# Sigmoid attention and a swish MLP on one core: layer one by seven products of halves, layer two in the same form, attention paced by batch

## The chip, the cores and the metric

One Trainium2 chip, one core. The metric is the device time of one execution in microseconds (us), as the median of several runs; the profile is of one further execution, on the same core. The engines are called by their short names: PE (TensorE, matrix products), DVE (VectorE), ACT (ScalarE), POOL (GpSimd, which also issues the casting loads) and SP (which issues the stores).

## The reference

```python
batch, n_heads, seq, head_dim = (8, 12, 448, 64)
n_tokens, d_model, d_ff = (3584, 768, 2048)

def _attn_ref(q, k, v):
    scale = 1.0 / np.sqrt(q.shape[-1])
    scores = scale * np.matmul(q, k.transpose(0, 1, 3, 2)) - np.log(S)
    attn = 1.0 / (1.0 + np.exp(-scores))
    return np.matmul(attn, v).astype(np.float32)

def _moe_ref(x, w_in, w_out, beta):
    h = x @ w_in
    g = h * (1.0 / (1.0 + np.exp(-beta * h)))
    return (g @ w_out).astype(np.float32)
```

Attention's output, heads side by side, is x: 8 batches of 448 tokens with 768 features. "Layer one" is h and g, 2048 features; "layer two" is the product with w_out, back to 768. All tensors come in float32; products run in float16 with float32 sums.

## The kernel before

**Attention.** Four heads are one quad, three quads a batch, 24 in all. A quad's q and k are loaded by POOL (tile `raw`), turned by DVE (`qT`, `kT`), and scored in visits (L218 on): one visit is 8 or 16 small products into two score tiles, which ACT turns into weights (`attnT`, L211, 128x896 at a time). There are two score tiles, so a visit's products wait for the sigmoids of the visit before. `attend` (L250 on) multiplies the weights of a whole quad by v, 16 products, and DVE casts the two results into `xT`, the batch's x with features on partitions.

**Layer one** (`dense1`, L280 on). For each of 16 blocks of 128 hidden features: six products of 128x128 weights by 448 tokens into one PSUM bank, one ACT sigmoid with beta as scale (L292), one DVE multiply of bank and sigmoid into `gt` (L295). In batch 0 the tokens are taken in two halves of 224. `gt` holds the hidden features of two batches.

**Layer two.** Tiles of 128 tokens. Tiles 0, 1, 2 and 27 are done directly (`dense2`, 16 products of 384 columns per half of the output). The others are done in pairs by Strassen's scheme (`strassen`, L377 on): the pair's hidden features, split in two halves, are a 2x2 matrix of blocks, w_out is another, and seven block products take the place of eight. Its weight sums (`weight_sum`) are made once by DVE, its five hidden sums per pair by DVE as they come up (L385), and the products are combined by DVE in `osb` (L415, L420) with one copy by ACT (L418).

**Banks.** PSUM has eight banks: four for the two score tiles, four single ones handed out by `bank`, the least recently used first. A product that has to stay open holds its bank by name (`held`) until `release`.

**Order.** The program order of every engine is written by hand. Attention's visits are the frame; between them stand units of a list, `fill` (layer one of a batch, then layer two of the tiles that it completes), each with an estimated cost in us. A visit is followed by units until their cost reaches a goal; the goals are a fixed list for the first visits (`spread`) and after them one rate for all. A batch's layer one has a first quad from which on it may start (`ready`). `attend` takes two banks, so units are run ahead of it until few enough are held. Engines run their queues in order; a wait holds back all that stands behind it on that engine.

The steps of the prediction touch `dense1` and its lines L284, L292, L295; `strassen`, L385 to L420; `attend` and L275; `bank`, `held`; `fill_units`, and the loop over visits at the end.

Of the kernel before, what the change touches and what calls it, by code (L numbers as in the profile page):

```python
# [13 lines left out]
def kernel(  # L14
# [17 lines left out]
    P = 128  # L32
# [23 lines left out]
    qTp = ctx.enter_context(tc.tile_pool(name="qTp", bufs=4))  # L56
    kTp = ctx.enter_context(tc.tile_pool(name="kTp", bufs=4))
    attnp = ctx.enter_context(tc.tile_pool(name="attnp", bufs=12))
    xTp = ctx.enter_context(tc.tile_pool(name="xTp", bufs=3))
    sump = ctx.enter_context(tc.tile_pool(name="sump", bufs=3))  # L60
    sigp = ctx.enter_context(tc.tile_pool(name="sigp", bufs=3))
# [31 lines left out]
    beta_in = const.tile([BLK, P], FP32, name="beta_in")  # L93
# [115 lines left out]
    def weigh(sco, n: int):  # L209
        at = attnp.tile([P, 2, S], FP16, tag="attnT", name="attnT")  # L210
        nc.scalar.activation(  # L211
            out=at[:, :, 0:n],
            in_=sco[:, :, 0:n],
            func=AF.Sigmoid,
            bias=NEG_LOG_S,
            scale=MSCALE,
        )
        return at  # L218
# [18 lines left out]
    def half_visit(g: int, c0: int, second: int):  # L237
# [13 lines left out]
        ats = {id(sco): weigh(sco, n) for sco, n in zip(scos, widths)}  # L251
# [53 lines left out]

    def dense2(t: int, half: int, part: int):
        last = t == NT - 1
        mid = 512 if last else HALF
        lo, hi = (0, mid) if half == 0 else (mid, DM)
        if part == 0:  # L310
            m2s[t, half] = bank("m2_ps", hi - lo, (t, half))
        m2 = m2s[t, half]
        for dc in range(part * NDC // N2, (part + 1) * NDC // N2):
            nc.tensor.matmul(  # L314
                m2,
                gt[:, dc, cols(t)],
                w_out16[:, dc, lo:hi],
                start=(dc == 0),
                stop=(dc == NDC - 1),
            )  # L320
        if part < N2 - 1:
            return
        release((t, half))
        if half == 0:
            osbs[t] = outp.tile([P, DM], FP32, tag="osb", name="osb")
        osb = osbs[t]
        nc.vector.tensor_copy(out=osb[:, lo:hi], in_=m2)  # L327
        if last:
            store(t, lo, hi)
        elif half == 1:  # L330
            store(t, 0, DM)
# [3 lines left out]
    def cols(t: int):  # L335
# [3 lines left out]

    ND = NDC // 2  # L340
    B11, B12, B21, B22 = (
# [4 lines left out]
    ws = {  # L346
        name: const.tile([P, ND, HALF], FP16, name=f"w_{name}")
        for name in ("T1", "T3", "T4", "T6", "T7")
    }

    def weight_sum(name: str, part: int):
        x, y, op = {
            "T1": (B11, B22, ALU.add),
            "T3": (B12, B22, ALU.subtract),
            "T4": (B21, B11, ALU.subtract),
            "T6": (B11, B12, ALU.add),
            "T7": (B21, B22, ALU.add),
        }[name]
        rows = slice(part * ND // 2, (part + 1) * ND // 2)
        nc.vector.tensor_tensor(out=ws[name][:, rows], in0=x[:, rows], in1=y[:, rows], op=op)  # L360
# [4 lines left out]

    def product(t: int, i: int):
        A11, A12, A21, A22 = hid(t, 0), hid(t, 1), hid(t + 1, 0), hid(t + 1, 1)
        return (
            ("r", A11, None, None, ws["T3"]),
            ("a", A22, None, None, ws["T4"]),  # L370
            ("s", A11, A12, ALU.add, B22),
            ("b", A21, A22, ALU.add, B11),
            ("a", A11, A22, ALU.add, ws["T1"]),
            ("r", A21, A11, ALU.subtract, ws["T6"]),
            ("a", A12, A22, ALU.subtract, ws["T7"]),
        )[i]

    NPROD = 7
    sums = {}

    def hidden_sum(t: int, i: int):
        _, x, y, op, _ = product(t, i)
        if op is not None:
            sums[t, i] = sump.tile([P, ND, P], FP16, tag="sum", name="sum")
            nc.vector.tensor_tensor(out=sums[t, i], in0=x, in1=y, op=op)  # L385

    def strassen(t: int, i: int, part: int):
        name, x, _, op, w = product(t, i)
        if part == 0 and i + 2 < NPROD:
            hidden_sum(t, i + 2)  # L390
        first = (t, name) not in m2s
        if first:
            m2s[t, name] = bank("m2_ps", HALF, (t, name))
        m2 = m2s[t, name]
        for dc in range(part * ND // 2, (part + 1) * ND // 2):
            nc.tensor.matmul(  # L396
                m2,
                (x if op is None else sums[t, i])[:, dc],
                w[:, dc],
                start=first and dc == 0,  # L400
                stop=(dc == ND - 1),
                skip_group_check=i >= 4,
            )
            first = False if dc else first
        if part == 0:
            return
        if i == 0:
            for u in (t, t + 1):
                osbs[u] = outp.tile([P, DM], FP32, tag="osb", name="osb")
        L, R = slice(0, HALF), slice(HALF, DM)  # L410
        o1, o2 = osbs[t], osbs[t + 1]
        r, a = m2s.get((t, "r")), m2s.get((t, "a"))

        def add(out, in0, in1, op=ALU.add):
            nc.vector.tensor_tensor(out=out, in0=in0, in1=in1, op=op)  # L415

        if i == 1:
            nc.scalar.copy(out=o2[:, L], in_=a)  # L418
        elif i == 2:
            nc.vector.tensor_copy(out=o1[:, L], in_=m2)  # L420
            add(o1[:, R], r, o1[:, L])
            release((t, "s"))
        elif i == 3:
            add(o2[:, L], m2, o2[:, L])
            release((t, "b"))
        elif i == 4:
            add(o2[:, R], a, o2[:, L], ALU.subtract)
        elif i == 5:
            add(o2[:, R], r, o2[:, R])
            release((t, "r"))  # L430
            store(t + 1, 0, DM)
        elif i == 6:
            add(o1[:, L], a, o1[:, L], ALU.subtract)
            release((t, "a"))
            store(t, 0, DM)
# [16 lines left out]
    M1_US, M1H_US, M2_US, LEAST_US = 1.13, 0.58, 2.6, 2.0  # L452


    def second_layer(tiles):
        for t in tiles:
            if t < 3 or t == NT - 1:
                for half in range(2):
                    for part in range(N2):
                        yield M2_US / N2, lambda a=(t, half, part): dense2(*a), False  # L460
            elif t % 2:
                for i in range(NPROD):
                    for part in range(2):
                        yield M2_US / 4, lambda a=(t, i, part): strassen(*a), i in (2, 3) or (i, part) == (4, 0)

    def filler_stream():
        for c0 in (0, QH):
            for dc in range(NDC):
                if c0 and dc == 10:
                    for part in range(N2):  # L470
                        yield M2_US / N2, 0, lambda part=part: dense2(0, 0, part), False
                yield M1H_US, 0, lambda dc=dc, c0=c0: dense1(0, dc, c0, QH), False
        for t, half in ((1, 0), (2, 0), (0, 1), (1, 1), (2, 1)):
            for part in range(N2):
                yield M2_US / N2, 0, lambda a=(t, half, part): dense2(*a), False
        for b in range(1, B):
            for dc in range(NDC):
                yield M1_US, QPB * (b + 1), lambda b=b, dc=dc: dense1(b, dc), False
            ends = [((x * S // P) - 1) // 2 * 2 + 1 for x in (b, b + 1)]
            for cost, unit, opens in second_layer(range(ends[0], NT if b == B - 1 else ends[1])):  # L480
                yield cost, 0, unit, opens

    fill = list(filler_stream())
    at_fill = [0]

    def fill_units(n: int):
        for _ in range(n):
            fill[at_fill[0]][2]()
            at_fill[0] += 1

# [3 lines left out]
    with tc.manual_schedule():  # L494
# [5 lines left out]
        still = const.tile([P, 512], FP16, name="still")  # L500
        nc.vector.memset(still, 0.0)
        nc.vector.memset(beta_in, 0.0)
# [64 lines left out]
        for g in range(QPB + 1, NQUAD, 2):  # L567
# [4 lines left out]
        spread += [2.95] * (sum(g < 4 * QPB for g, _, _ in visits) - len(spread))  # L572

        total = sum(u[0] for u in fill[at_fill[0] :])
        tail = 16 * M1_US + 9.6 * M2_US
        rest = (total - sum(spread) - tail) / (len(visits) - len(spread))
        adds = {
            5: [("T4", 0)],
            6: [("T4", 1)],
            8: [("T3", 0)],  # L580
            9: [("T3", 1), ("T1", 0)],
            10: [("T1", 1), ("T6", 0)],
            11: [("T6", 1)],
            12: [("T7", 0)],
            13: [("T7", 1)],
        }
        budget, spent = 0.0, 0.0
        for i, (g, jt, also) in enumerate(visits):
            if jt == 0:
                if g > QPB:  # L590


                    while len(held) > 1 and (len(held) > 2 or fill[at_fill[0]][3]):
                        spent += fill[at_fill[0]][0]
                        fill_units(1)
                    attend(g - 1, 0, S)
                if g + 2 < NQUAD:
# [9 lines left out]
            for name, part in adds.get(i, ()):  # L607
                weight_sum(name, part)
            budget += spread[i] if i < len(spread) else rest
# [6 lines left out]
            goal = max(budget, spent + LEAST_US) if g > QPB + 2 else budget  # L616
            while at_fill[0] < len(fill):
                cost, ready, _, _ = fill[at_fill[0]]
                if ready > g or spent + cost / 2 > goal:
                    break  # L620
                spent += cost
                fill_units(1)
        attend(NQUAD - 1, 0, S)
        fill_units(len(fill) - at_fill[0])
# [30 lines left out]
```

## Time and profile before

| | us |
|---|---|
| median of three runs | 387.97 (387.73 to 388.02) |
| profiled execution | 388.37 |
| its span, first to last instruction | 386.6 |
| layer-one products, 448 columns, 672 of them (L284) | 134.2 busy |
| attention sigmoids (L211), 171 of them | 145.2 busy |
| layer-one sigmoids (L292), 144 of them | 84.4 busy |
| POOL elementwise work | none but four small fills |

Busy time of PE is that of overlapping instructions: one product of 448 columns is shown as 353 ns while the next starts 189 ns after it. Starts, not durations, give PE's pace. The busy share of another engine is an average over stages: ACT is at 59% over the span and three quarters in layer one beside attention.

### The profile page before, as it was taken

The numbers are of one execution on the slowest core, as the hardware profiler recorded it, in microseconds if no ns is written. First come the engines' busy times: TensorE is split into PE (matmuls) and PEld (weight loads), VectorE is DVE, ScalarE is ACT, GpSimd is POOL, SyncE is SP. The second block draws the span as 40 slices with busy tenths as digits, with TensorE's granted clock in tenths as the row PEclk, the third lists the DMA queues.
The fourth block names the chain that finished last, engine by engine and source line by source line (L and its number), as shares of the span: only waits on it lengthen the run. The fifth ranks groups of instructions, "written<-read, shape, count | busy, mean of one in ns | idle before, by whom it ended". The sixth has DMA issues, their size and how long they took to land.

```text
span 386.6 us, 7375 instructions
## 1 busy us (share of the span) xinstructions
PE 381.2 (99%) x2991; PEld 191.4 (50%) x2991; DVE 231.5 (60%) x437; ACT 228.8 (59%) x329; POOL 67.3 (17%) x116
## 2 busy tenths in 40 slices
PE   8999999999999999999999999999999999999996
PEld 2478754444544444444554445544455444555563
DVE  2356364885766656565765667655686565645762
ACT  3987755687374795497364783467762677525200
POOL 7833353131110410140110410104100000000000
DMA  7999999728353850555363561639203300030033
GB/s 111 174 190 203 197 205 198 163 59 96 49 110 70 130 72 0 123 71 57 49 126 75 83 70 28 129 73 129 36 13 83 83 1 2 0 83 0 2 81 122
DMA packets 42401, 34.30 MB, mean 89 GB/s; under 512 B 21872, under 2 KB 38784, under 8 KB 42368
## 3 DMA queue, kind: packets, MB, share of 16 engines
q0 software_dynamic: 36976, 22.81, 43.6%
q1 hardware_dynamic: 5392, 11.02, 10.9%
q8 instruction: 23, 0.38, 0.4%
q14 instruction: 10, 0.08, 0.1%
HBM read 45.62 MB, written 11.01 MB: 146 GB/s over the span
## 4 chain that ended last, share of the span: by engine, by line
PE 95%; ACT 2%; DMA 1%; issue 1%; DVE 1%; POOL 0%; ACTq 0%; POOLq 0%
PE m_ps L284 38%; PE m_ps L396 29%; PE sco L200 12%; PE av_ps L266 10%; PE m_ps L314 5%; ACT attnT L211 2%; DMA raw<-in_k_dram 1%; PE idle_ps L507 1%; DVE xT L275 0%; POOL raw L110 0%; DVE kT L186 0%; ACT sg L292 0%; DVE osb L327 0%; DVE gt L295 0%; ACTq L292 0%
## 5 line engine op out<-in xcount | busy, mean ns | idle before, releaser
L211 ACT ACTIVATE attnT<-sco 128x896 f16<-128x896 f32 (+1 forms) x171 | 145.2, 902 | 89.1 <-PE sco L200 88.3
L284 PE MATMUL m_ps<-xT,w_in 128*128 128x448 f16 (+1 forms) x864 | 154.7, 332 | 0.2 <-DVE gt L295 0.2
L295 DVE TENSOR_TENSOR gt<-m_ps,sg 128x448 f16<-128x448 f32 (+1 forms) x144 | 81.7, 572 | 81.1 <-ACT sg L292 77.2
L284 PEld LDWEIGHTS <-w_in 128*128 128x128 f16 x864 | 80.6, 98 | 70.7 <-issue 15.3
L292 ACT ACTIVATE sg<-m_ps,beta_sb 128x448 f32<-128x448 f32 (+1 forms) x144 | 84.4, 596 | 36.3 <-PE m_ps L284 31.0
L396 PEld LDWEIGHTS <-sum 128*128 128x128 f16 x480 | 45.2, 98 | 36.2 <-issue 7.9
L200 PE MATMUL sco<-qT,kT 32*128 32x448 f16 (+3 forms) x864 | 52.2, 340 | 0.9 <-DVE kT L186 0.5
L396 PE MATMUL m_ps<-w_T,sum 128*128 128x384 f16 x288 | 51.6, 327 | 0.0
L110 POOL DMA_DIRECT2D raw<-in_q_dram x27 | 14.9, 553 | 186.5 <-DVE kT L190 180.2
L415 DVE TENSOR_TENSOR osb<-m_ps,osb 128x384 f32<-128x384 f32 x60 | 33.3, 555 | 18.7 <-PE m_ps L396 16.9
L266 PE MATMUL av_ps<-attnT,v 128*64 128x448 f16 (+3 forms) x432 | 42.1, 341 | 0.0
L275 DVE CAST xT<-av_ps 128x448 f16<-128x448 f32 (+1 forms) x54 | 28.8, 567 | 18.2 <-PE av_ps L266 18.2
L385 DVE TENSOR_TENSOR sum<-gt 128x1024 f16<-128x1024 f16 x60 | 39.1, 677 | 0.1
L396 PE MATMUL m_ps<-w_T,gt 128*128 128x384 f16 x192 | 34.2, 327 | 0.0
L396 PE MATMUL m_ps<-w_out,sum 128*128 128x384 f16 x192 | 33.7, 326 | 0.0
L266 PEld LDWEIGHTS <-v 128*64 128x64 f16 (+1 forms) x432 | 19.0, 108 | 24.6 <-issue 17.6
L200 PEld LDWEIGHTS <-kT 32*128 32x128 f16 (+1 forms) x864 | 13.5, 96 | 29.2 <-issue 27.0
L396 PEld LDWEIGHTS <-gt 128*128 128x128 f16 x192 | 18.1, 98 | 14.7 <-issue 3.1
L314 PE MATMUL m_ps<-w_out,gt 128*128 128x384 f16 (+2 forms) x128 | 22.5, 327 | 0.0
L131 POOL DMA_DIRECT2D v<-in_v_dram x32 | 19.8, 635 | 10.4 <-DMA w_in<-in_moe_w_in_dram 5.9
L178 DVE STREAM_TRANSPOSE qT<-raw 128x448 f32<-128x448 f32 (+1 forms) x27 | 16.6, 616 | 7.4 <-DMA raw<-in_q_dram 7.4
L314 PEld LDWEIGHTS <-gt 128*128 128x128 f16 x128 | 11.9, 98 | 10.3 <-issue 3.1
(23 smaller groups left out, 97.2 us busy)
## 6 DMA issues: line engine op xcount, KB each, us to landing
out_dram<-osb SPq DMA_DIRECT2D x98, 96.0 KB, 1.9
raw<-in_k_dram POOLq DMA_DIRECT2D x24, 224.0 KB, 4.7
raw<-in_q_dram POOLq DMA_DIRECT2D x21, 224.0 KB, 3.7
v<-in_v_dram POOLq DMA_DIRECT2D x32, 144.0 KB, 6.1
w_in<-in_moe_w_in_dram POOLq DMA_DIRECT2D x8, 384.0 KB, 10.9
w_out<-in_moe_w_out_dram POOLq DMA_DIRECT2D x4, 768.0 KB, 13.9
v<-in_v_dram POOLq DMA_DIRECT2D x16, 48.0 KB, 6.0
out_dram<-osb SPq DMA_DIRECT2D x2, 384.0 KB, 2.3
```

What stands on the lines that cost most here:

```text
L131: nc.gpsimd.dma_start(out=vs[b][i * BLK : (i + 1) * BLK, :, 0:JF].rearrange("p h j d -> p h (j d)"), in_=rows[:, :, JF * i * D : JF * (i + ...
L200: nc.tensor.matmul(sco[base : base + nk, hh, u0 : u0 + n], kT[g][lo : lo + BLK, jt * P : jt * P + nk, e], qT[g][lo : lo + BLK, c0 : c0 + n ...
L211: nc.scalar.activation(out=at[:, :, 0:n], in_=sco[:, :, 0:n], func=AF.Sigmoid, bias=NEG_LOG_S, scale=MSCALE,)
L266: nc.tensor.matmul(av[hh * D : (hh + 1) * D, 0:n], vs[b][base : base + nk, 2 * (s % NPAIR) + hh, jt], at[base : base + nk, hh, 0:n], start ...
L275: nc.vector.tensor_copy(out=xTs[b][:, s % NPAIR, c0 : c0 + n], in_=av[:, 0:n])
L284: nc.tensor.matmul(m1[:, 0:n], w_in16[:, hc, dc * P : (dc + 1) * P], xTs[b][:, hc, c0 : c0 + n], start=(hc == 0), stop=(hc == NHC - 1),)
L292: nc.scalar.activation(out=sg[:, 0:n], in_=m1[:, 0:n], func=AF.Sigmoid, bias=0.0, scale=beta_sb[:, dc : dc + 1])
L295: nc.vector.tensor_tensor(out=gt[:, dc, off : off + n], in0=m1[:, 0:n], in1=sg[:, 0:n], op=ALU.mult)
L314: nc.tensor.matmul(m2, gt[:, dc, cols(t)], w_out16[:, dc, lo:hi], start=(dc == 0), stop=(dc == NDC - 1),)
L385: nc.vector.tensor_tensor(out=sums[t, i], in0=x, in1=y, op=op)
L396: nc.tensor.matmul(m2, (x if op is None else sums[t, i])[:, dc], w[:, dc], start=first and dc == 0, stop=(dc == ND - 1), skip_group_check= ...
L415: nc.vector.tensor_tensor(out=out, in0=in0, in1=in1, op=op)
```

## The change

**Layer one of batches 2 to 7** (`wino1`). The features of x (768) and the tokens of a batch (448) are each cut in two halves, and so are the hidden features (2048). One 2x2 by 2x2 block product then takes seven products of halves (Winograd's form) in place of eight. A batch is four blocks d; each block makes 2 x 128 hidden features of the upper half and the same of the lower half by seven units in the order P1, P6, P5, P7, P2, P3, P4. A unit is six products of 224 columns. Four token sums (`token_sum`, DVE) are made per batch, queued in `side` and taken one after each unit, all of them ahead of P6. Four weight sums S1 to S4 are made once, S3 in the place of a block of w_in.

Three banks stay open across units: P2 adds to P1's bank, P3 to P5's, P4 to P7's. ACT copies P1 into an `osb` tile; DVE adds P6, P5, P7, P3 and P4 to what stands there. The sigmoids are on halves (two of 224 after P2, two of 224 after P3) and two of 448 after P4; one multiply of a block is DVE's, three are POOL's.

**Layer two** (`wino2`) is in the same form and order: four hidden sums a pair in place of five, five DVE adds, two ACT copies in place of one copy each by ACT and DVE. The pairs are 4-5 to 26-27, the direct tiles 0 to 3; T1 takes the place of a block of w_out. The last pair is stored in halves.

**Pacing.** From batch 2 on the goals rise evenly to the point at which the next batch's attention ends: two units before its layer one begins.

**Room.** `qT` and `kT` have 3 buffers (4 before), `attnT` 9 (12), `sg` 4 (3). Four of batch 0's attention tiles lie in `osb` tiles, and `still` and `beta_in` in other tiles.

```diff
-    qTp = ctx.enter_context(tc.tile_pool(name="qTp", bufs=4))
-    kTp = ctx.enter_context(tc.tile_pool(name="kTp", bufs=4))
-    attnp = ctx.enter_context(tc.tile_pool(name="attnp", bufs=12))
+    qTp = ctx.enter_context(tc.tile_pool(name="qTp", bufs=3))
+    kTp = ctx.enter_context(tc.tile_pool(name="kTp", bufs=3))
+    attnp = ctx.enter_context(tc.tile_pool(name="attnp", bufs=9))
...
+    ORDER = ("P1", "P6", "P5", "P7", "P2", "P3", "P4")
+    BANK = {"P1": "x", "P2": "x", "P6": "y", "P5": "w", "P3": "w", "P7": "z", "P4": "z"}
+    OPENS = ("P1", "P6", "P5", "P7")
...
+    def token_sum(b: int, i: int):
...
+        out, in0, in1 = (
+            (t[:, 0], b12, b11),
+            (t[:, 1], b22, t[:, 0]),
+            (b12, b22, b12),
+            (t[:, 2], b21, t[:, 1]),
+        )[i]
+        add(out, in0, in1, ALU.subtract)
...
+    def wino1(b: int, d: int, p: str):
+        while p == "P6" and side:
+            side.pop(0)()
...
+            "P1": lambda: (A11, x[:, 0:NK, 0:QH]),
+            "P2": lambda: (A12, x[:, NK:NHC, 0:QH]),
+            "P3": lambda: (S4, x[:, NK:NHC, QH:S]),
+            "P4": lambda: (A22, t[:, 2]),
+            "P5": lambda: (S1, t[:, 0]),
+            "P6": lambda: (S2, t[:, 1]),
+            "P7": lambda: (S3, x[:, 0:NK, QH:S]),
...
+        if opens:
+            m2s[key] = bank("m1_ps", S, key)
+        m = m2s[key].rearrange("p (q n) -> p q n", q=2)
+        for j in range(2):
+            for hc in range(NK):
+                nc.tensor.matmul(
+                    m[:, j],
+                    lhs[:, hc, (2 * d + j) * P : (2 * d + j + 1) * P],
+                    rhs[:, hc],
...
+        if p == "P1":
+            nc.scalar.copy(out=oa[:, 0], in_=m)
+        elif p == "P6":
+            add(oa[:, 0], m, oa[:, 0])
+        elif p == "P5":
+            add(oa[:, 1], m, oa[:, 0])
+        elif p == "P7":
+            add(oa[:, 1], m, oa[:, 1])
+        elif p == "P2":
+            for j in range(2):
+                sigmoid(ob[:, 1, j], m[:, j], 2 * d + j)
+        elif p == "P3":
+            add(ob[:, 0], m, oa[:, 0])
+            sg = sigp.tile([P, S], FP32, tag="sg", name="sg").rearrange("p (q n) -> p q n", q=2)
+            for j in range(2):
+                sigmoid(sg[:, j], ob[:, 0, j], 2 * d + j)
+            nc.gpsimd.tensor_tensor(
+                out=gt[:, 2 * d : 2 * d + 2, off + QH : off + S], in0=ob[:, 0], in1=sg, op=ALU.mult
+            )
+        elif p == "P4":
+            add(oa[:, 0], m, oa[:, 0])
+            first = m2s[b, d, "x"].rearrange("p (q n) -> p q n", q=2)
+            nc.vector.tensor_tensor(
+                out=gt[:, 2 * d : 2 * d + 2, off : off + QH], in0=first, in1=ob[:, 1], op=ALU.mult
+            )
+            release((b, d, "x"))
+            for j in range(2):
...
+                sigmoid(sg, oa[:, :, j], dc)
+                nc.gpsimd.tensor_tensor(
...
+        if p not in ("P1", "P5", "P7", "P2"):
+            release(key)
...
+        if p == "P1":
+            nc.scalar.copy(out=o2[:, L], in_=m2)
+        elif p == "P6":
+            add(o2[:, L], m2, o2[:, L])
+        elif p == "P5":
+            add(o2[:, R], m2, o2[:, L])
...
+        elif p == "P2":
+            nc.scalar.copy(out=o1[:, L], in_=m2)
...
+    def attended(g: int):
+        b, t = divmod(g, QPB)
+        if b > 1 and t == QPB - 1:
+            side.extend(lambda i=i: token_sum(b, i) for i in range(4))
...
-        spread += [2.95] * (sum(g < 4 * QPB for g, _, _ in visits) - len(spread))
-
-        total = sum(u[0] for u in fill[at_fill[0] :])
-        tail = 16 * M1_US + 9.6 * M2_US
-        rest = (total - sum(spread) - tail) / (len(visits) - len(spread))
...
+        for b in range(2, B):
+            knot = [v[:2] for v in visits].index((QPB * (b + 1), 0)) if b < B - 1 else len(visits)
+            n, at = knot - len(goals), goals[-1]
+            goals += [at + (starts[QPB * (b + 1)] - at) * (j + 1) / n for j in range(n)]
```

## The prediction

> **What bounds the kernel now.** I read the busy shares first, then the chain of waits, then the timeline of TensorE, and only then the other engines in the stages that the change rebuilds.
>
> ```profile
> PE 381.2 (99%) x2991; PEld 191.4 (50%) x2991; DVE 231.5 (60%) x437; ACT 228.8 (59%) x329; POOL 67.3 (17%) x116
> ...
> PE 95%; ACT 2%; DMA 1%; issue 1%; DVE 1%; POOL 0%; ACTq 0%; POOLq 0%
> ```
>
> TensorE (PE) is busy all the time and the chain that ends last is 95% PE. A busy PE need not be at full pace, so I take its pace from starts in its timeline:
>
> ```profile
> 39.51 2.47 PE L284 MATMUL m_ps<-xT,w_in 128*128 128x224 f16 x24
> 41.91 0.57 PE L200 MATMUL sco<-qT,kT 32*128 32x448 f16 x8
> 42.42 1.32 PE L284 MATMUL m_ps<-xT,w_in 128*128 128x224 f16 x12
> 43.58 0.65 PE L314 MATMUL m_ps<-w_out,gt 128*128 128x384 f16 x3
> ...
> 341.79 18.32 PE L284 MATMUL m_ps<-xT,w_in 128*128 128x448 f16 x96
> 359.94 2.76 PE L396 MATMUL m_ps<-w_T,gt 128*128 128x384 f16 x16
> ```
>
> Start to start, 96 products of 448 columns take 18.15 us: 0.189 us each. Those of 224 columns exist too (batch 0): 12 in 1.16 us, 0.097 each, and 24 in 2.40 us, 0.100 each with the 0.1 us in it that every switch to a score block costs. So half the columns cost about half, and nothing waits. The cover is in two windows: layer one of batch 3 between its score blocks, and of batch 7 alone.
>
> ```profile
> 122.60:148.70 26.10, 26.10 (x197) 11.53 (x197) 14.86 (x27) 19.94 (x29) 5.80 (x10) 1.00 0.62 93
> 341.80:360.00 18.20, 18.20 (x98) 9.43 (x97) 9.62 (x16) 9.50 (x15) 0.00 (x0) 1.00 0.12 28
> ```
>
> The columns are span, PE, weight loads, VectorE (DVE), ScalarE (ACT), POOL, clock, DMA. ACT is already 19.9 of 26.1 us in layer one with attention: three quarters. It hides because each layer-one unit needs one sigmoid and one multiply and then frees its bank.
>
> **The change, step by step.**
> (1) PE work. Batches 2 to 7 lose 6 x 96 = 576 products of 448 columns, 576 x 0.189 = 108.9 us, and gain 6 x 4 x 7 x 6 = 1008 of 224. At 0.096 (between the two rows, the switch taken off) that is 96.8 us: **-12.1 us**. Bounds: at 0.100 -8.1, at 0.0954 ((2.40 - 0.11)/24) -12.7. Layer two has seven products of the same size before and after, and the four tiles done directly are 0 to 3 in place of 0 to 2 and 27: nothing.
>
> The Trainium skill ("TensorE: Matmul & The Clock Gate", section "LDWEIGHTS (loading the stationary operand)") gives a weight load of P columns as P / 1.2 ns, an estimate of 107 ns for 128, more than a half product streams; were that the pace, the new products would take 107.5 us and the gain be 1.4. The trace has 24 such pairs in 2.40 us, so the loads overlap here and the rule does not bind.
>
> (2) ACT, per d (one block of seven products; four to a batch). Before, four sigmoids of 448. After: copy of P1 (the 384 copy takes 0.48; 0.53 for 448), two sigmoids of 224 after P2, two after P3, two of 448 after P4. Queue spacing, from runs in the rows: 224 0.34 (four in 1.47 us), 448 0.53, attention's 896 0.81 (two in 1.72).
>
> ```profile
> 134.65 0.63 ACT L292 ACTIVATE sg<-m_ps,beta_sb 128x448 f32<-128x448 f32 x1 [0.50 <-PE m_ps L284]
> 135.18 1.72 ACT L211 ACTIVATE attnT<-sco 128x896 f16<-128x896 f32 x2
> 136.77 1.39 ACT L292 ACTIVATE sg<-m_ps,beta_sb 128x448 f32<-128x448 f32 x2
> ```
>
> Sum 0.43 + 4 x 0.34 + 2 x 0.53 = 2.85 us per d, 11.4 a batch (8.5 before). In the built program's order four to six score blocks stand among a batch's 28 units, each with 1.62 us of ACT: about 20 us of ACT in a section whose PE work is 16.1 + 5 x 0.52 + 1.57 (one attend) = 20.2. **ACT becomes full where PE is full.**
>
> (3) The chain through one d. P2 adds to the bank that the copy of P1 reads; P3 to the bank of P5, after P5's add; P4 to that of P7. So PE itself waits now. ACT is in order: the next d's copy stands behind the P4 sigmoids of this one. From P4's last product to the next P3: drain 0.17 (a product's 0.35 less its slot of 0.19), add 0.62 (the 448 row of L295, 624 ns), two sigmoids 1.06, copy 0.53, add 0.62, add 0.62, four hand-overs of 0.03 (364.05 + 0.56 to 364.64): 3.74 us. PE has P1, P6, P5, P7, P2 to do meanwhile, 2.87. **It stands 0.87 us per d**, less 0.5 if a score block falls in between; and then two attention sigmoids (1.62) may stand in ACT's queue ahead of the copy.
>
> I walked the queues by hand in the built order with these durations. Batch 7, alone, from P1 of d0 at 1.30: copy 2.04 to 2.57; P3 at 5.24; P4 ends 6.39; its sigmoids 7.31 to 8.37; copy 8.90; P6's add 9.55, P5's 10.2; P3 at 10.24. So 5.0 us from P3 to P3 in place of 4.03, three times. Batch 4, with scores behind P6: d0's P4 sigmoids leave ACT at 6.51, the score block's two at 8.13, the copy ends at 8.66; P2 wanted 7.33 and goes at 8.70, P3 waits again to 10.0; d2 and d3 lose 0.5 to 1.3 each.
>
> (4) Token sums. P6 needs two of the four (672 elements; 1024 take 0.677, 1536 take 0.932, hence 0.50). They stand behind attend's two casts (1.16). With two units of layer two and P1 as cover P6 still waits 0.5 to 1.3 a batch. In the last batch a hidden sum adds 0.75 before layer two.
>
> Waits by batch, with (3) and (4): b2 3.0, b3 4.1, b4 5.5, b5 4.1 (the order of b3), b6 2.4, b7 4.9: **+24.0**.
>
> (5) Costed at nothing: six more weight sums (932 ns each) beside batch 1, where DVE is busy 16.0 of 23.7 us (window 75.0 to 98.7); without cover 5.6. Three multiplies a d on POOL: no row shows one; the same shape takes 0.62 on DVE and ACT's longest row is 0.915, and up to 1.34 each they fit in 4.03; I take 0.9 by the nearer engines. Queued behind them on POOL are the loads of raw and v, each issue 0.55 to 0.63 and landing in 4 to 6 us, a quad (some 12 us) before use; if POOL is late, the transposes on DVE are next and then the adds. The shorter rings (attnT 9, kT and qT 3) still hold a quad and the visit after it. osb is shared with layer two; d1 reuses tiles whose stores (1.9 us to land) left about 4 us earlier: nothing, 1 us a batch if not. I left the transposes (1.45 us a quad on DVE) out of the walk, 0 to 1 a batch more.
>
> The Trainium skill ("SBUF — State Buffer", section "SBUF: two separate sides") says that a VectorE instruction with two SBUF inputs and a GpSimd instruction that reads SBUF exclude each other for a whole instruction. No row here can show it; with "GPSIMD Engine Reference", section "Elementwise — side-by-side cycle accounting" (4497 ns for 2048 elements, an estimate of 0.98 for 448), two hidden sums behind a batch's last d would each wait up to 1 us, at most 12 us over six batches.
>
> Sum on the span: 386.6 - 12.1 + 24.0 = 398.5. Around the span the profiled execution has 388.37 - 386.6 = 1.8: 400.3. It stands 0.4 above the median of the runs, so **400 us**.
>
> **Rivals.**
> A, the forecast: ACT's queue and the chain hold PE, 394 to 407. For it: the 19.9 of 26.1 above, and the order of the queue. Against: it adds many short waits.
> B, only the floor of the chain: ACT never queues the scores ahead of a copy at a bad moment. Then 0.35 at 15 places where a score block helps, 0.87 three times in b7, 5.7 for the sums: 13.6. 388 - 12.1 + 13.6 = 389.5; 388.8 to 394. Against it: in b3, b4 and b5 the built order has scores right before a copy.
> C, PE stays the bound, and it is faster. Place: ACT's run from P4's sigmoids to the next copy. Their inputs are in SBUF, which no row has. If run and adds are 0.36 us shorter than 3.74 (0.87 in b7), no d waits; what stays are the token and hidden sums, 5.7: 388 - 12.1 + 5.7 = 381.6; 377 to 387. Above 3.38 us of chain it is A or B. For it: a queue that begins with half idle ACT in layer two can catch up there. Against: 24 d's use it.
> D, the product does not do what it says: at 0.100 per half product the gain is 8.1 and A gives 404; with POOL over 1.34 us per multiply or late loads, past 407.
>
> **How the numbers follow.** A 0.50, B 0.17, C 0.25, D 0.08. The likeliest is A's 400, its own range 394 to 407. To leave out no more than 2 in 10, I go down into C: 381 to 407. 0.2% is 0.8 us, what this measurement can tell from no change (the runs spread 0.3). Faster is C, 0.25; the same is the lower edge of B, 0.03; slower 0.72.
>
> **What would show it.** PE with idle time released by the ACT copy (before P2) and by DVE adds (before P3), 0.5 to 1.4 us each, in the windows of layer one only; P3 to P3 in the last batch 5.0 us; ACT over 90% busy in layer one with attention; half products at 0.096 where nothing waits. Wrong, if PE is still 99% busy there, or if the idle time is released by POOL or DMA.

## The result, and the profile after

The changed kernel takes 416.74 us (median of four runs, 414.57 to 417.51) against 388.0 before: 1.0733 times as long, interval 1.0689 to 1.0777. That is 28.8 us slower, where the forecast said 12 us slower with 407 as its upper end. The profiled execution took 417.42, its span 415.6.

From the page of the changed kernel: busy shares, TensorE's granted clock in 40 slices, and the chain that ended last by engine.

```profile
PE 382.1 (92%) x3423; PEld 232.8 (56%) x3423; DVE 267.4 (64%) x491; ACT 252.4 (61%) x413; POOL 152.6 (37%) x188
...
PEclk9999999999999999989998999989999999999999
...
PE 59%; DVE 13%; ACT 11%; DMA 9%; issue 5%; POOL 2%; SPq 0%; DVEq 0%; ACTq 0%; POOLq 0%
```

PE went from 99% busy to 92%, and from 95% of the chain to 59%: it is no longer the only bound. Three slices show a lowered clock; before had none. Who made PE wait is in the view of waits (engine, tile and line that waited, who released it: us in total, times, longest).

```profile
PE m_ps L424 <- DVE osb L350: 14.1, 18, 1.9
PE m_ps L516 <- DVE sum L350: 5.4, 5, 1.4
PE m_ps L424 <- DVE xs L350: 3.5, 6, 1.0
PE m_ps L424 <- ACT osb L445: 2.6, 3, 1.3
...
PE m_ps L424 <- DVE gt L466: 0.8, 4, 0.3
```

L424 is a product of layer one, L516 one of layer two. The first row is P3 or P4 behind the DVE adds; the fourth is P2 behind the copy of P1; the third is P6 behind the token sums; the second is layer two's P6 behind a hidden sum; the fifth is P5, waiting for P1's bank behind DVE's multiply. All five are new. The last batch alone, in PE's timeline (start, duration, count, idle before):

```profile
364.12 1.31 PE L424 MATMUL m_ps<-xT,w_in 128*128 128x224 f16 x12
365.27 0.74 PE L424 MATMUL m_ps<-xT,w_S 128*128 128x224 f16 x6
...
370.53 0.73 PE L424 MATMUL m_ps<-xT,w_S 128*128 128x224 f16 x6 [0.65 <-DVE osb L350]
...
375.86 0.73 PE L424 MATMUL m_ps<-xT,w_S 128*128 128x224 f16 x6 [0.65 <-DVE osb L350]
...
385.38 0.82 PE L516 MATMUL m_ps<-w_T,sum 128*128 128x384 f16 x4 [1.41 <-DVE sum L350]
```

The rows of `xT` and `w_S` with six products are P3: 365.27, 370.53, 375.86 are 5.3 us apart, where the products between them need 4.03. Where nothing waits, the half products run at the forecast's pace (12 from 364.12 to 365.27, 0.096 each).

The idle column leaves out how a product drains, so I also took the time from start to start of PE's rows and subtracted count x pace (0.189, 0.1625 and 0.096 us a product of 448, 384 and 224 columns; 0.063 a product for a score block of 8, 0.53 in all for one of 16; 0.098 for attend's). What is over, by the wait that stands there, in us of the profiled execution:

| | before | after | e2 | e7 | e11 | e12 |
|---|---|---|---|---|---|---|
| P2, P3, P4 of layer one | 0 | 20.1 | 7.8 | 5.6 | 3.6 | 0 |
| P6 behind token sums | 0 | 4.5 | 4.5 | 1.2 | 1.2 | 0 |
| layer two's P6 behind hidden sums | 0 | 6.0 | 6.6 | 0 | 0 | 0 |
| attend, and P5 for a bank | 1.1 | 6.8 | 5.1 | 12.9 | 10.0 | 1.5 |
| before 95 us | 7.4 | 7.0 | 6.5 | 7.1 | 7.1 | 6.5 |
| rest (small rests, slow products) | 4.4 | 8.4 | 5.9 | 8.4 | 7.0 | 4.0 |
| sum | 13.0 | 52.9 | 36.4 | 35.1 | 29.0 | 12.0 |

Nearly the whole loss is here: 52.9 less 13.0 is 39.9 us of new waits, and 39.9 less the forecast's 12.1 of PE work is 27.8 of the 29.0 by which the span grew. (Of the other 1.2, 0.8 stands behind the last product: from its start to the end of the span it is 4.2 us, before 3.4.) The columns e2 to e12 are the experiments below; sums are of unrounded numbers.

### The profile page after: what moved, and what is told of

Read it like the earlier page. It is cut to its first block, busy times and chain, and to the rows that moved or that the text cites. A ratio compares the mean times of both kernels' runs of the same rounds, so it can differ in the third digit from the quotient of the medians.

```text
span 415.6 us, 8633 instructions
## 1 busy us (share of the span) xinstructions
PE 382.1 (92%) x3423; PEld 232.8 (56%) x3423; DVE 267.4 (64%) x491; ACT 252.4 (61%) x413; POOL 152.6 (37%) x188
## 4 chain that ended last, share of the span: by engine, by line
PE 59%; DVE 13%; ACT 11%; DMA 9%; issue 5%; POOL 2%; SPq 0%; DVEq 0%; ACTq 0%; POOLq 0%
PE m_ps L516 25%; PE m_ps L424 10%; PE av_ps L272 9%; DVE osb L350 8%; PE sco L200 7%; ACT sg L440 5%; PE m_ps L290 5%; DMA w_out<-in_moe_w_out_dram 5%; ACT attnT L212 4%; PE m_ps L321 4%; DMA w_in<-in_moe_w_in_dram 2%; ACT osb L445 2%; DMA raw<-in_k_dram 2%; DVE sum L350 1%; DVE gt L466 1%
## 5 line engine op out<-in xcount | busy, mean ns | idle before, releaser
L350 DVE TENSOR_TENSOR osb<-m_ps,osb 128x448 f32<-128x448 f32 (+1 forms) x180 | 107.8, 600 | 80.1 <-PE m_ps L516 34.8
L460 POOL TENSOR_TENSOR gt<-osb,sg 128x448 f16<-128x448 f32 x24 | 27.3, 1138 | 171.3 <-ACT sg L440 166.0
L440 ACT ACTIVATE sg<-osb,beta_sb 128x224 f32<-128x224 f32 (+1 forms) x96 | 48.9, 569 | 23.1 <-DVE osb L350 22.6
L424 PEld LDWEIGHTS <-w_in 128*128 128x128 f16 x576 | 54.2, 98 | 14.6 <-issue 13.7
L474 POOL TENSOR_TENSOR gt<-osb,sg 128x448 f16<-128x448 f32 x48 | 58.5, 1239 | 5.4 <-ACT sg L440 3.7
L516 PEld LDWEIGHTS <-sum 128*128 128x128 f16 x384 | 35.9, 98 | 35.3 <-DVE sum L350 8.1
L424 PEld LDWEIGHTS <-w_S 128*128 128x128 f16 x432 | 41.1, 99 | 25.8 <-issue 21.6
L424 PE MATMUL m_ps<-xT,w_in 128*128 128x224 f16 x432 | 51.1, 261 | 2.6 <-ACT osb L445 2.6
L281 DVE CAST xT<-av_ps 128x448 f16<-128x448 f32 (+1 forms) x54 | 28.8, 567 | 29.0 <-PE av_ps L272 28.9
L516 PE MATMUL m_ps<-w_T,sum 128*128 128x384 f16 x192 | 35.9, 327 | 5.4 <-DVE sum L350 5.4
L290 PE MATMUL m_ps<-xT,w_in 128*128 128x224 f16 (+1 forms) x288 | 40.3, 291 | 0.2 <-DVE gt L301 0.2
L516 PEld LDWEIGHTS <-gt 128*128 128x128 f16 x288 | 27.1, 98 | 21.4 <-issue 4.8
L424 PE MATMUL m_ps<-xs,w_S 128*128 128x224 f16 x288 | 34.4, 262 | 4.8 <-DVE xs L350 3.5
L516 PE MATMUL m_ps<-w_out,sum 128*128 128x384 f16 x192 | 35.5, 327 | 0.0
L516 PE MATMUL m_ps<-w_out,gt 128*128 128x384 f16 x192 | 35.5, 327 | 0.0
L272 PEld LDWEIGHTS <-v 128*64 128x64 f16 (+1 forms) x432 | 20.3, 111 | 25.9 <-issue 20.1
L290 PEld LDWEIGHTS <-w_in 128*128 128x128 f16 x288 | 26.2, 98 | 13.4 <-issue 4.9
L301 DVE TENSOR_TENSOR gt<-m_ps,sg 128x224 f16<-128x224 f32 (+1 forms) x48 | 21.8, 468 | 18.4 <-ACT sg L298 17.5
L424 PE MATMUL m_ps<-xT,w_S 128*128 128x224 f16 x144 | 18.4, 266 | 12.2 <-DVE osb L350 12.2
```

The costliest lines, as they stand in the source:

```text
L272: nc.tensor.matmul(av[hh * D : (hh + 1) * D, 0:n], vs[b][base : base + nk, 2 * (s % NPAIR) + hh, jt], at[base : base + nk, hh, 0:n], start ...
L281: nc.vector.tensor_copy(out=xTs[b][:, s % NPAIR, c0 : c0 + n], in_=av[:, 0:n])
L290: nc.tensor.matmul(m1[:, 0:n], w_in16[:, hc, dc * P : (dc + 1) * P], xTs[b][:, hc, c0 : c0 + n], start=(hc == 0), stop=(hc == NHC - 1),)
L301: nc.vector.tensor_tensor(out=gt[:, dc, off : off + n], in0=m1[:, 0:n], in1=sg[:, 0:n], op=ALU.mult)
L424: nc.tensor.matmul(m[:, j], lhs[:, hc, (2 * d + j) * P : (2 * d + j + 1) * P], rhs[:, hc], start=opens and j == 0 and hc == 0, stop=hc == ...
L440: nc.scalar.activation(out=out, in_=in_, func=AF.Sigmoid, bias=0.0, scale=beta_sb[:, dc : dc + 1])
```

## The experiments

All times are medians; "before" ran beside each group and took 387.6 to 388.0. The theory: ACT's queue is in order, and the next block's copy of P1 stands behind this block's P4 sigmoids, which stand behind DVE's adds; that ring holds PE. The rivals: it is the new layer two, the pacing or the rings; it is POOL's multiplies; it is too many score blocks in layer one.

**The copy of P1 ahead of P4's sigmoids.** Nothing is left out; the two sigmoids and their multiplies are issued after the next block's copy.

```diff
+            while late:
+                late.pop()()
             nc.scalar.copy(out=oa[:, 0], in_=m)
...
-            for j in range(2):
+            def gate():
+                for j in range(2):
...
+            late.append(gate)
+            if d == ND // 2 - 1:
+                late.pop()()
```

> In layer one the two sigmoids (and POOL multiplies) of P4 are issued behind the next block's copy of P1 in ACT's queue; nothing else moves. Theory: P3 to P3 in batch 7 falls from 5.33 us to 4.0 to 4.4, in the other batches ACT's copy comes 1.1 us earlier at 15 places, and the time falls by 12 to 22 us, to 395 to 405. Rival (POOL's multiplies and its exclusion of DVE set the pace): batch 7 stays at 5.2 to 5.4 and the time at 413 to 418. Rival (ACT is full in the sections with attention, the order in its queue doesn't matter): batch 7 gets shorter by 3 to 4 us and nothing else, 411 to 414.

Measured: 401.14 us (400.95 to 401.61), ratio 1.0352 (1.0337 to 1.0368): 15.6 us less than the changed kernel, by order alone. The reason is seen in ACT's timeline of the changed kernel in batch 4, and then in PE's at the same place:

```profile
220.51 1.98 ACT L440 ACTIVATE sg<-osb,beta_sb 128x224 f32<-128x224 f32 x4 [0.45 <-DVE osb L350]
222.39 1.69 ACT L212 ACTIVATE attnT<-sco 128x896 f16<-128x896 f32 x2
223.99 0.52 ACT L445 COPY osb<-m_ps 128x448 f32<-128x448 f32 x1
```

```profile
224.56 0.73 PE L424 MATMUL m_ps<-xT,w_in 128*128 128x224 f16 x6 [1.26 <-ACT osb L445]
225.94 1.18 PE L424 MATMUL m_ps<-xT,w_S 128*128 128x224 f16 x6 [0.65 <-DVE osb L350]
227.05 2.77 PE L272 MATMUL av_ps<-attnT,v 128*64 128x448 f16 x16
```

ACT is never idle from 220.5 to 224.5: four sigmoids (two of 224 after P3 and two of 448 after P4, which the view merges under the first shape), two of attention, and only then the copy. P2 waits 1.26 us for it, P3 another 0.65 for the adds after it. (Attend then takes 2.77 us in place of 1.64: the clock, last section.) In the other order, batch 7 of e2 on PE and ACT:

```profile
351.46 0.74 PE L425 MATMUL m_ps<-xT,w_S 128*128 128x224 f16 x6
...
355.90 0.74 PE L425 MATMUL m_ps<-xT,w_S 128*128 128x224 f16 x6
...
369.01 1.47 PE L524 MATMUL m_ps<-w_T,sum 128*128 128x384 f16 x8 [1.56 <-DVE sum L350]
```

```profile
353.66 0.51 ACT L446 COPY osb<-m_ps 128x448 f32<-128x448 f32 x1
354.07 1.23 ACT L441 ACTIVATE sg<-osb,beta_sb 128x448 f32<-128x448 f32 x2
```

The copy now leads the two sigmoids of 448, P3 to P3 is 4.44 us and P3 waits for nothing; what is over 4.03 is P5, waiting for P1's bank behind DVE's multiply (0.16 to 0.32 us idle in each of the three blocks). ACT does the same work (251.6 us busy, 252.4 in the changed kernel). It was the place in the queue, not the amount. The hidden sum at the end is untouched: 1.56.

**Layer one by eight products again, all else as changed.** This is the rival that layer two, pacing or rings cost the time; the weight and token sums of layer one go too.

```diff
+            for dc in range(NDC):
+                units.append(Unit(M1_US, ready, lambda b=b, dc=dc: dense1(b, dc)))
...
-        names = [(n, i) for n in ("S1", "S2", "S4", "T3", "T2", "T4") for i in range(2)]
+        names = [(n, i) for n in ("T3", "T2", "T4") for i in range(2)]
```

> Layer one of batches 2 to 7 is put back to eight products (16 units of six 448-column products and one sigmoid, one multiply); layer two's new form, the pacing and the smaller rings stay. If all of the loss sits in layer one's chain of seven units (my theory), this is within 2 us of before, 386 to 390. If the pacing, the layer-two form or the smaller rings cost part of it, it stays well above, 392 to 405.

Measured: 395.9 us (394.41 to 397.87), ratio 1.0219 (1.0184 to 1.0253). Layer one carries most of the loss, but the 8 us left were a miss of the theory. Two things make them: layer two's P6 waits for hidden sums in three places (2.8 us idle), and an artefact of the edit: with the S sums gone, T3 moved to an early visit, DVE stood 3.5 us for w_out's load and the transposes behind it came late.

**POOL's multiplies left out.**

```diff
-                sigmoid(sg, oa[:, :, j], dc)
-                nc.gpsimd.tensor_tensor(
...
+                sigmoid(gt[:, dc, off : off + S].rearrange("p (h n) -> p h n", h=2), oa[:, :, j], dc)
```

> POOL's three multiplies per block are left out: the sigmoids write the hidden features directly, so the lower half and half of the upper half are gates alone; DVE's multiply stays. Theory (ACT's copy in its queue and the adds): POOL is off the path, time falls by 2 to 6 us at most (the hidden sums that now take 864 ns return to 680, and the wait of 1.0 to 1.4 us before layer two's P6), 410 to 415. Rival (POOL's 1.14 to 1.24 us multiplies pace layer one): P3 to P3 in batch 7 falls to 4.1 and the time to 395 to 403.

Measured: 410.53 us (409.73 to 411.19), ratio 1.059 (1.057 to 1.061): 6.2 less. PE never waits for POOL in the changed kernel, so how can POOL cost 6? The rows of the hidden sums on DVE, first of the changed kernel, then without the multiplies (duration min/median/max in ns):

```profile
L350 DVE TENSOR_TENSOR sum<-gt x24: 651/683/1649, 134.2 to 403.7; 128x1024 f16<-128x1024 f16 x24
L350 DVE TENSOR_TENSOR sum<-sum,gt x12: 676/872/1076, 135.9 to 403.1; 128x1024 f16<-128x1024 f16 x12
```

```profile
L350 DVE TENSOR_TENSOR sum<-gt x24: 648/681/686, 134.3 to 397.0; 128x1024 f16<-128x1024 f16 x24
L350 DVE TENSOR_TENSOR sum<-sum,gt x12: 675/680/681, 136.0 to 396.4; 128x1024 f16<-128x1024 f16 x12
```

The same instruction takes up to 1.65 us while POOL multiplies, and never over 0.69 without. The wait of layer two's P6 fell from 5.4 to 3.2 us idle. The rest of the 6.2 is not one wait. P3's waits in layer one gave some, and so did the granted clock: it is 0.985 in the changed kernel's profile, with three stretches of 3.41 us at half (last section), and 1.0 in this one. Against the changed kernel's one run at a clock of 0.999, 414.57, the difference is 4.0.

**Fewer score blocks in layer one.**

```diff
-    W1_US, W2_US = 0.573, 0.653
+    W1_US, W2_US = 0.3, 0.653
```

> The cost of a layer-one unit in the pacing is set to 0.3 in place of 0.573, so that fewer visits fall into layer one: four in place of five or six per batch, the others into layer two. Theory (ACT's queue, attention's sigmoids ahead of the copy): 1 to 2 us less per batch, 406 to 413. Rival (only the chain of one block counts): blocks without a score block wait longer, no gain, 415 to 420.

Measured: 420.19 us (419.32 to 420.76), ratio 1.084 (1.0824 to 1.0857): 3.5 more. A miss: attention beside layer one is not, on balance, what the stage suffers from; it fits the forecast's own remark that a score block covers 0.5 us of a block's wait.

**What is left over e2.** Three edits on top of it, each nothing but order: score blocks in layer one only between P6 and P5 (e6); the first pair's hidden sums three units earlier, and four units of layer two, not two, between attention's end and layer one (e7); both, with DVE's multiply moved up behind P3's add (e8). Beside them, e1 with the early hidden sums (e9).

```diff
-                if unit.ready > g or spent + unit.cost / 2 > goal:
+                if unit.ready > g or (unit.stop and spent + unit.cost / 2 > goal):
```

> On top of the version with the copy ahead of P4's sigmoids: visits may stand in layer one only between P6 and P5, so that attention's two sigmoids never stand right ahead of the copy of P1 in ACT's queue. Theory: the seven waits of PE ahead of P3 (6.1 us) and the slow ones beside them go, 393 to 397. Rival (ACT is full there whatever the order): no gain, 399 to 403.

Measured: 399.09 us (399.0 to 399.69), ratio 1.0298 (1.0281 to 1.0315): 2.0 less, where more was expected. What P4 gained, the score blocks' own waits took back (1.9 us behind attention's sigmoids, 0.3 before).

```diff
-                units[at - 2].after.append(lambda t=t: hidden_sum(t, 0))
-                units[at - 1].after.append(lambda t=t: hidden_sum(t, 1))
+                back = (5, 3) if early else (2, 1)
+                early = False
+                for i in range(2):
+                    units[at - back[i]].after.append(lambda t=t, i=i: hidden_sum(t, i))
...
-                starts[unit.ready] = done - 2 * W2_US
+                starts[unit.ready] = done - 4 * W2_US
```

> On top of the version with the copy ahead of P4's sigmoids: the first two hidden sums of a batch's first pair are issued three units earlier, and four units of layer two in place of two stand between attention's end and layer one. Theory (sums come too late for P6): the waits on hidden sums (5.9 us) and on token sums (3.5 us) go, 391 to 395. Rival (DVE is full, the sums only push the adds back): 398 to 402.

Measured: 398.29 us (397.3 to 399.19), ratio 1.0272 (1.0246 to 1.0298): 2.9 less, where both kinds of sums together cost PE 11.1 us in the table. They are gone as forecast (1.2 us of token sums left, no hidden sum), but the time came back on the same engine elsewhere. PE's waits in e7:

```profile
PE m_ps L425 <- DVE osb L350: 4.1, 9, 0.7
PE av_ps L272 <- DVE osb L350: 3.6, 3, 1.8
PE m_ps L425 <- DVE gt L469: 3.3, 9, 0.6
```

The second row is attend, waiting up to 1.8 us for a bank that DVE's adds had still to empty; the third is P5 waiting for its bank behind DVE's multiply. DVE was late by the same work; it was only asked for something else next.

> Both of the above together, and DVE's multiply of a block directly behind P3's add, so that P1's bank is free one unit earlier. If the waits are separate and add up: 383 to 388, below or at before. If they share one cause (DVE or ACT full): 390 to 396.

Measured: 406.35 us (402.8 to 407.42), ratio 1.0465 (1.0414 to 1.0515): worse than each of its parts. Its profile, taken of the fastest of its runs (402.8), shows where:

```profile
PE sco L200 <- ACT attnT L212: 7.3, 12, 1.4
```

Score blocks that may not stand in most of layer one stand one behind another in layer two, and there wait for the sigmoids of the one before.

> Layer one as before (eight products), layer two's new form and the pacing, with the first two hidden sums of a batch's first pair issued three units earlier. Theory (the 8 us that the new layer two and pacing cost are waits on hidden sums): 389 to 392. Rival (the smaller rings of qT, kT and attnT, or the first 75 us): stays at 394 to 397.

Measured: 393.07 us (390.48 to 393.57), ratio 1.0124 (1.009 to 1.0158). The hidden sums' waits are gone; the late transpose of e1's own edit stays (2.7 us idle, the longest wait of its profile).

**The two that were left: the banks, and POOL.** On e7: DVE's multiply behind P3's add, with attend only between blocks (e10); and POOL's multiplies left out (e11).

```diff
-                    while len(held) > 1 and (len(held) > 2 or fill[at_fill[0]].opens):
+                    while held and (
+                        fill[at_fill[0]].cost == W1_US
+                        or len(held) > 2
+                        or len(held) > 1 and fill[at_fill[0]].opens
+                    ):
```

> On top of the version with the copy ahead and the sums early: DVE's multiply of a block directly behind P3's add, and attend in layer one only between blocks, where no bank is held. Theory (the waits left are separate hand-overs of banks: 3.3 us on P1's bank, 3.6 us of attend on banks): 391 to 395. Rival (DVE's queue is the bound, so the multiply only pushes P4's add back): 397 to 401.

Measured: 400.49 us (399.88 to 401.04), ratio 1.0326 (1.0311 to 1.0342): 2.2 more. A miss. The multiply now stands ahead of P4's add on DVE, and PE's wait for the adds in layer one went from 4.1 to 6.8 us; attend's fell from 4.1 to 2.3 (for adds and multiply together). The two edits were not tried apart.

> The version with the copy ahead and the sums early, POOL's three multiplies per block left out (the sigmoids write the hidden features directly). It prices POOL where ACT's queue is no longer first. Theory (DVE's two-input sums wait for POOL's multiplies, 1.08 in place of 0.68 us each, little more): 394 to 397. Rival (with the copy out of the way POOL is the next bound): 386 to 391.

Measured: 393.5 us (393.4 to 393.64), ratio 1.0147 (1.0132 to 1.0162): 4.8 less than e7. Here no hidden sum holds PE any more, and POOL's multiplies still cost 4.8: through DVE being late for banks (4.1 to 2.6, 3.6 to 1.6 and 3.3 to 2.8 us in the three rows above, 4.0 together), and through the clock. Two of e7's four runs, at a clock of 0.994, took 399.2, the two at 0.999 and 1.0 took 397.3 and 397.4; against these the multiplies cost 3.9.

**The floor.** e9 with the weight sums begun four visits later, so that e1's artefact is gone.

```diff
-        adds = dict(enumerate(names, 4))
+        adds = dict(enumerate(names, 8))
```

> Layer one as before, layer two's new form, pacing and early hidden sums, with the weight sums begun four visits later, so that DVE doesn't wait for the second half of w_out at 55 us (my own edit had moved them up). Theory (nothing else of layer two, pacing or rings costs time): 387.5 to 390. Rival (pacing or rings): 391 to 394.

Measured: 389.16 us (388.99 to 389.54), ratio 1.0038 (1.0024 to 1.0053). New layer two (with its first hidden sums early), pacing and rings cost 1.4 us and no more; PE is 98% busy, and the one new wait of PE in its profile is attend's for a copy of v, 0.3 us.

**Seven products where attention is out of the way.** e12 with `wino1` in batch 7 alone, copy ahead.

```diff
-            for dc in range(NDC):
-                units.append(Unit(M1_US, ready, lambda b=b, dc=dc: dense1(b, dc)))
+            if b < B - 1:
+                for dc in range(NDC):
+                    units.append(Unit(M1_US, ready, lambda b=b, dc=dc: dense1(b, dc)))
...
+            elif b == B - 1:
+                for d in range(ND // 2):
+                    for p in ORDER:
```

> Seven products in layer one of batch 7 alone, the one batch that has no attention beside it; batches 2 to 6 go by eight products, layer two, pacing and rings are the new ones, weight sums from the ninth visit, hidden sums early, P1's copy ahead of P4's sigmoids, and the multiply behind P3's add is VectorE's. Theory (the chain costs less where ACT and VectorE are not shared with the attention): 2.1 us less products, less 1.0 to 1.5 us of waits, so 387.8 to 389.0, that is 0.3 to 1.3 below the 389.16 of the same kernel with eight products in all batches. Rival (the chain alone costs as much as it saves, whatever runs beside it): 389.5 to 391.

Measured: 390.04 us (389.84 to 390.77), ratio 1.0057 (1.0043 to 1.007): not under e12, as the theory had it, but at it or a little above (the intervals of the ratios overlap). Batch 7's 28 units run from 337.86 to 356.42, 18.56 us, where eight products took 18.15 before. Two waits have a name:

```profile
339.17 1.32 PE L425 MATMUL m_ps<-xs,w_S 128*128 128x224 f16 x12 [0.57 <-DVE xs L350]
...
355.85 0.73 PE L425 MATMUL m_ps<-xs,w_in 128*128 128x224 f16 x6 [0.72 <-DVE osb L350]
```

The products themselves are 28 x 6 x 0.096 = 16.1 us, so 2.4 stand, counted from start to start: 0.7 and 0.9 at these two, and about 0.8 in rests of 0.1 to 0.2 at P4 and P6, too short for the view to name. The first of the two is the token sums. The second is P4 behind P7's add, and DVE's queue shows why that add is late:

```profile
354.21 1.06 DVE L350 TENSOR_TENSOR sum<-gt 128x1024 f16<-128x1024 f16 x1
355.19 0.61 DVE L350 TENSOR_TENSOR osb<-m_ps,osb 128x448 f32<-128x448 f32 x1
```

P7's products are done by 354.0, but its add waits behind a hidden sum of layer two, moved early and itself slow beside a multiply of POOL. So alone and in the better order the scheme still takes what the missing eighth product saves, but through its sums: the ring of copies, adds and multiplies has at most the 0.8 of the rests. A version with these two sums out of the way was not tried.

No version ran faster than the kernel before. Between e2 and it, 401.1 down to 387.8, the runs show 2.9 (sums earlier), 4.8 (POOL's multiplies, the clock with them), 4.3 (the rest of layer one's scheme, e11 against e12) and 1.4 (layer two, pacing and rings). That the multiplies could be done without that price was not tried.

## Why the prediction was right, and where it was not

The direction was right, the size was not: +12 was forecast, +28.8 came. By its own steps:

(1) *PE work, -12.1.* Right: 0.096 us a half product, in every stretch where nothing waits; with the waits of the table, 27.8 of the span's 29.0 us are accounted for.

(2) and (3) *ACT's queue and the chain: of the 24.0, what is left when rival B's 5.7 for the sums are taken off, 18.3.* The mechanism was right, and e2 shows it: the in-order place of the copy. The table's 20.1 is near the size. A block alone took 5.32 us from P3 to P3 (365.27 to 381.22 is three), not 5.0: dependent adds follow each other at 0.73 us (three in 2.08), not 0.65. One sentence in it was wrong: "ACT becomes full where PE is full". Windows of the changed kernel, batch 4 (span, PE, weight loads, DVE, ACT, POOL, clock, DMA):

```profile
213.00:230.00 17.00, 14.60 (x138) 9.62 (x134) 11.26 (x22) 10.40 (x18) 4.63 (x5) 0.90 0.21 48
230.00:247.00 17.00, 15.02 (x161) 10.38 (x154) 12.36 (x22) 14.57 (x25) 8.71 (x9) 1.00 0.18 28
```

ACT is at 61% and 86%, not over 90%: it waits in the ring like the others. The sign that I had named for the step did not come, though the step held.

(4) *Sums, 5.7: a hidden sum of 0.75 in the last batch only, so 4.9 of token sums.* Token sums: 4.5, right. **Hidden sums: 6.0 in five places.** This is the first term that was mis-sized. I counted the wait only where no attention follows; it stands at most passages from layer one to layer two. DVE's timeline in batch 2 of the changed kernel:

```profile
134.22 0.68 DVE L350 TENSOR_TENSOR sum<-gt 128x1024 f16<-128x1024 f16 x1
134.82 0.62 DVE L350 TENSOR_TENSOR osb<-m_ps,osb 128x448 f32<-128x448 f32 x1
135.36 0.62 DVE L466 TENSOR_TENSOR gt<-m_ps,osb 128x448 f16<-128x448 f32 x1
135.89 1.07 DVE L350 TENSOR_TENSOR sum<-sum,gt 128x1024 f16<-128x1024 f16 x1
```

P4's add and the multiply stand between the two sums that P6 needs, and the second sum takes 1.07 us, beside POOL's multiply that runs from 135.28 to 136.42. P6 starts at 137.02, 0.80 late.

(5) *Costed at nothing.* Six weight sums: right (before 95 us, 7.0 against 7.4). Rings and stores: no wait of PE names them. **Attend's and P5's banks were not in the sum at all: 5.7 us over before**; of it attend at half clock, 2.77 and 2.90 us in place of 1.64, is 2.4. **POOL:** 1.14 and 1.24 us a multiply where I took 0.9; they fit, as argued, and behind 95 us no wait of PE, DVE or ACT names a load. But their price is not on POOL. The rule of the Trainium skill ("SBUF — State Buffer", section "SBUF: two separate sides"), which the prediction quoted and left out of its sum, holds here: sums of two SBUF inputs and the multiplies hold each other up (figures in the last section). Leaving the multiplies out was worth 6.2 us, 2.2 of them at the hidden sums, where at most 12 had been estimated by it. **The clock**, not thought of at all: 4.0 in the row "rest", most of it slow products.

So the step that failed is the sum of waits, 24.0 against 39.9. The chain and the token sums make 24.6 of it where 23.2 were forecast; 5.3 of the excess are hidden sums, 5.7 banks and attend, 4.0 the rest (and -0.4 the early part). Each was a term at nothing, or nearly, and the range's upper end, 407, had been drawn with them at nothing too.

The rivals: B (only the chain's floor, 388.8 to 394) needs an ACT that never queues badly; even with the copy moved, the kernel took 401. C (PE stays the bound) asked for a chain 0.36 us shorter; e2 shortens it by more than that, and sums and banks take the place: the case had counted 5.7 us for them, and they are 16 in e2's column. D lies nearest in time, but neither of its conditions came: the pace was 0.096, the multiplies under 1.34 on average, the loads in time.

## What to carry to other kernels

Before a scheme trades products for sums, set the saving per block beside the length of the ring that it builds through in-order queues: here 0.5 us a block were saved, and with no attention beside it and in the better order the waits of ring and sums still took 0.6 a block, most of it the sums. In such a ring the first thing to change is the order: the short instruction that the bound engine waits for goes ahead of the long ones that nobody waits for yet (15.6 us here, at no cost). And a term that is set at nothing on a busy engine needs an upper bound in the range: time taken off one wait of a late engine came back at its next (9.9 us of waits for sums removed gave 2.9).

## What was not expected of the hardware

**Short gaps halve the clock for 3.4 us.** Half-microsecond windows of the changed kernel around the attend of 2.77 us (columns as above; the clock is the third number from the end):

```profile
225.50:226.00 0.50, 0.06 (x1) 0.05 (x1) 0.40 (x2) 0.50 (x2) 0.00 (x0) 1.00 0.00 0
226.00:226.50 0.50, 0.50 (x4) 0.43 (x4) 0.50 (x1) 0.11 (x1) 0.00 (x0) 0.59 0.00 0
226.50:227.00 0.50, 0.50 (x4) 0.16 (x2) 0.12 (x1) 0.00 (x0) 0.00 (x0) 0.50 0.00 0
...
229.00:229.50 0.50, 0.50 (x8) 0.07 (x4) 0.00 (x0) 0.00 (x0) 0.50 (x1) 0.50 0.00 0
229.50:230.00 0.50, 0.50 (x13) 0.17 (x12) 0.13 (x1) 0.00 (x0) 0.50 (x2) 1.00 0.00 0
```

From 226.1 to 229.5, 3.41 us, the granted clock is 0.50, after PE had been idle 1.26 and 0.65 us within 3.4. It happens twice more, at 178 (1.13 and 0.71 idle before it) and at 270 (one gap of 1.89). Gaps of 0.47 and 0.92 at 120 us did not do it, nor did a single one of 1.82 at 169, so the length of the gaps alone doesn't decide. The three falls, at 178.30, 226.09 and 270.46, lie 14 and 13 times 3.41 apart. In the stretches of 3.41 us that end at them PE is shown busy for 1.57, 1.50 and 1.52 us; in the one with the gap of 1.82, 168.06 to 171.48 on the same grid, for 1.60. That is a narrow difference, and in e7 a fall came after 1.65, so where the line lies is not shown. The Trainium skill ("TensorE: Matmul & The Clock Gate", section "What's actually happening") has two clocks, half and full, and windows of about 3.4 us; the trace agrees with both. It puts the fall after at least one idle window, about 3.4 us; here under 2 us of idle time in that stretch were enough, and the measurement decides. Over the changed kernel's runs the time goes with it: 414.57 us at a mean clock of 0.999, 416.05 at 0.992, 417.42 and 417.51 at 0.985 and 0.986. So PE's waits cost nearly 3 us more than themselves in some runs; the kernel before, with PE 99% busy, stayed at 1.0. The gain of 15.6 by e2's order has this in it: against 414.57 it is 13.4.

**Sums and multiplies that hold each other up.** In the changed kernel's profile DVE's hidden sums (two inputs in SBUF) take 0.65 to 0.69 us alone and 1.00 to 1.65 when they start during a multiply of POOL's; multiplies beside sums take up to 1.59 us where others take 1.12 to 1.24. DVE's adds with one input in PSUM stay at 0.58 to 0.63, beside multiplies or not.
